# Turning k and x by transposing products, and a written order of all instructions, in a linear-attention and gated-MLP kernel

## The chip, the cores and the metric

The kernel runs on one core of a Trainium2 chip. The metric is the time that the device takes for one execution of the program, in microseconds (us).

## The reference

A linear attention with decay runs over 4 batches, 8 heads and 768 steps with a head size of 48; its output, put together over the heads, goes through an RMS norm and a gated MLP (384 to 1536 and back).

```python
for t in range(S):
    state = alpha[:, :, t, :, None] * state + einsum('bhd,bhe->bhde', k[:, :, t], v[:, :, t])
    y[:, :, t] = einsum('bhd,bhde->bhe', q[:, :, t], state)
x = y.transpose(0, 2, 1, 3).reshape(B * S, H * D)
rms = sqrt(mean(x * x, axis=-1) + 1e-06)
xn = x / rms * rms_g
g = xn @ w_gate
out = (g * sigmoid(g) * (xn @ w_val)) @ w_out
```

All is float32. The gate and value weights are 384 by 1536, the output weights 1536 by 384.

## The kernel before, in words

The 3072 rows are cut into 24 chunks of 128 (six in time for each of four batches). `attention(cc)` makes one chunk: two scans of the decays on VectorE (L661) with a reciprocal between them (L681), the products kh (L691) and qp (two halves, L698), score products on TensorE (L768; for the four first chunks in float32, L778), a mask on VectorE (L784; L794 for the first chunks), value products (L856; L804 for the first chunks), products with the state (L835, L813) and state sums (L933, L908). Float32 matrices are split into a high and a low float16 part (the low parts are made on VectorE, for instance L705, L732, L723, L758, L886 and L1005), and three products of parts stand for one. Chunks 0 to 3 are each batch's first; they have no state before them and stay in float32. Their k is turned by `k_across` (L893) and their normed x by `x_across` (L981): matmuls whose moving operand is an identity matrix `one`. For x, `x_less` (L995) then subtracts the high part in the same PSUM tile. Later chunks turn k and x by transposing DMAs.

The MLP works on seven groups of chunks (4, 2, 2, 4, 4, 4, 4). `expert_in` multiplies a group with one of twelve blocks of gate and value weights (L1149), gates on VectorE (L1166), makes the high part on ScalarE (L502) and the low part on VectorE (L1179). `expert_out` multiplies with the output weights (L1219), copies out (L1230) and stores through SyncE (L1234). Weights come as 64-bit words whose bytes `decode` puts together on VectorE (L541, L544, L552) and ScalarE (L536, L502).

After all weights have come once more and been inspected, `verdict` forms a flag that tells whether the scaled splits were good for these inputs: two small matmuls on TensorE (L1367, L1394) with VectorE steps behind each, the last of them a reduction (L1396) and two tiny steps (L1399, L1407) that write `flag`. Each engine reads the flag (L1425) and branches (L1426). In the branch for good inputs stands the store of the last output tile, held back until then:

```python
bad = nc.values_load(flags[0], min_val=0, max_val=1)
with tc.If(bad > 0) as case:
    general(...)
with case.Else():
    last_store[0]()
```

The order of the work is the planner's. Every step is a `plan.op` with an engine, a cost, its forerunners (`deps`) and the tiles that it holds (`use`; `BUFS` says how many of each there are). `Plan.order` counts due times backwards through the forerunners, adds the tuned numbers of `LATE`, `W_LATE`, `DUE`, `GAP` and `PACE`, and then lets each engine take, of what could start next, the step with the earliest due time. The result is sorted by planned start, and each engine, the DMA queue on SyncE among them, gets its steps in that order. Where the plan leaves TensorE idle before 45 us, it adds filler matmuls (`warm`, L1329).

There are 1737 steps: 390 on TensorE, 717 on VectorE, 458 on ScalarE, 25 on GpSimd, 147 on SyncE. In the order before, the verdict's second matmul stands between the second and third of the four groups of output products of chunk 22, and its reduction before the last two output copies. The two pieces of chunk 1's loads are issued with the decays (261 KB) first and the rest (512 KB) three loads later.

Of the kernel before, what the change touches and what calls it, by code (L numbers as in the profile page):

```python
# [64 lines left out]
    abs=0.86, odd=0.57, cnt=1.0, wh=0.83, pow=0.8, sc=0.76, sc32=0.8, ys=0.42, ysw=0.38, yv=0.63, yvw=0.57, y32=1.12, add=0.5, take=0.4, u=0.5, po=1.48, xp=0.9, kp=1.15, u32=0.66,  # L65
# [10 lines left out]
PACE = [1.0, 1.0, 1.15, 1.18, 1.18, 1.18, 1.18]  # L76
GAP = [-15.7, 137.0, 36.9, 106.2, -22.7, -134.2, 399.9]
DUE = [
    -719.9, -428.4, 411.3, -551.6, 184.4, 443.0, 1038.8, 186.9, 211.3, 740.5, 1018.7, 654.7, 756.4,
    831.8, 770.0, 432.6, 1179.9, 1019.1, 1109.0, 512.2, 336.7, 338.7, 475.6, 483.2,  # L80
]
LATE = dict(
    a16=95.7, abs=95.5, add=-3.0, al=-37.8, cnt=239.3, dec=-143.8, gd=128.7, k16=-225.5, kb=-100.3,
    kh=211.5, kl=37.3, kp=-148.6, ld2=204.9, load=96.2, mask=-127.2, near=132.3, ob=-144.7,
    odd=-153.0, pow=73.9, q16=-96.0, qh=38.4, ql=-11.4, rec=52.2, rest=-69.8, rg=8.7, rgt=-201.8,
    rgw=-6.4, s16=44.3, sc=-125.2, sc32=-36.5, scan=303.9, sd=70.9, shift=-71.0, sl=-52.1, sq=109.6,
    st=-82.7, st0=-193.5, take=-59.8, u=-107.2, u32=-53.5, v=186.2, v16=124.3, vl=-14.9, wh=160.7,
    wid=-93.7, wl=-301.4, wl2=15.7, wneg=80.9, x=-230.4, x16=-36.5, x32=-16.4, xb=-7.0, xl=-43.5,
    xneg=126.0, xp=27.6, y32=-52.5, ys=-23.6, ys32=-78.8, ysw=-43.9, yv=-74.0, yvw=-116.3,
)  # L90
LATE_CHECK = 3
W_LATE = [
    -285.5, -492.0, -249.7, -250.4, -99.8, -149.6, -106.2, -73.2, 53.8, -132.7, 151.4, 126.2, 126.8,
    172.8, 286.5, 195.7, 182.1, 333.3,
]
WARM_UNTIL, WARM, WARM_FIRST = 45.0, 0.24, 14
CUTS = [0, 2, 4]
SIDE = [3, 1]


class Plan:
# [9 lines left out]
    def op(self, engine, cost, fn, deps=(), use=(), due=None, lock=False, kb=0, late=0.0, kind=None, tile=None):  # L111

        o = dict(e=engine, c=cost, fn=fn, d=[d for d in deps if d], u=tuple(use), due=due, lock=lock,
                 kb=kb, late=late, i=len(self.ops), n=[], k=kind, w=tile)
        for d in o["d"]:
            d["n"].append(o)
        for k in o["u"]:
            self.users[k] = self.users.get(k, 0) + 1
        self.ops.append(o)
        return o  # L120

    def order(self):
        for o in reversed(self.ops):
            lat = WAIT.get(o["e"], LOAD_LAG + LOAD_END + 1.5)
            due = [n["s"] - lat for n in o["n"]] + ([o["due"]] if o["due"] is not None else [])
            o["s"] = min(due, default=1e6) - o["c"]
        for o in self.ops:
            o["s"] += o["late"]
        free = {t: [(0.0, i) for i in range(n)] for t, n in BUFS.items()}
        held, left, last = set(), dict(self.users), {}  # L130
        engine = dict.fromkeys(("PE", "DVE", "ACT", "POOL", "SP"), 0.0)
        ready = {e: [] for e in engine}
        wait = {o["i"]: len(o["d"]) for o in self.ops}
        for o in self.ops:
            o["r"] = 0.0
            if not o["d"]:
                ready[o["e"]].append(o)
        bus, port, done = 0.0, 0.0, []

        owner = [None]  # L140

        def start(o):
            t = max(engine[o["e"]], o["r"])
            if o["lock"] and t < port and o["e"] != owner[0]:
                t = port
            want = {}
            for k in o["u"]:
                if k not in held:
                    want[k[0]] = want.get(k[0], 0) + 1
            for tag, n in want.items():  # L150
                f = sorted(free[tag])
                if len(f) < n:
                    return None
                t = max(t, f[n - 1][0])
            return t

        left_ops = len(self.ops)
        while left_ops:
            left_ops -= 1
            best = None  # L160
            for e, ops in ready.items():
                at = [(start(o), o) for o in ops]
                at = [x for x in at if x[0] is not None]
                if not at:
                    continue
                t0 = min(x[0] for x in at)
                t, o = min((x for x in at if x[0] <= t0 + 0.12), key=lambda x: (x[1]["s"], x[1]["i"]))
                if best is None or t < best[0]:
                    best = (t, o)
            assert best, "the plan is stuck"  # L170
            t, o = best
            e = o["e"]
            ready[e].remove(o)
            for k in o["u"]:
                if k not in held:
                    held.add(k)
                    free[k[0]].sort()
                    self.slot[k] = free[k[0]].pop(0)[1]
            cost = o["c"]
            if e == "PE" and t < WARM_UNTIL:  # L180
                n = int((t - engine[e] - 0.3) / WARM)
                at = [x[1] for x in free["mm"] if x[0] <= engine[e]]
                if n > 0 and at:
                    fn = lambda slot=at[0], n=n: self.warm(slot, n)
                    done.append(dict(o, c=n * WARM, t=engine[e], fn=fn, k="warm", w=None))
            if o["lock"]:
                port, owner[0] = t + cost, e
# [12 lines left out]
            for n in o["n"]:  # L200
                n["r"] = max(n["r"], t + cost if n["e"] == e else o["f"])
                wait[n["i"]] -= 1
                if not wait[n["i"]]:
                    ready[n["e"]].append(n)
# [140 lines left out]
def tile_attn_moe(  # L345
# [12 lines left out]
    nc = tc.nc  # L358
    NC, _, AW = att.shape
    R = 112  # L360
# [152 lines left out]
    def add(engine, kind, *args, **kw):  # L513
        w = kw.get("tile")
        late = LATE.get(kind, 0.0) + (W_LATE[w] if w is not None else 0.0)
        return op(engine, COST[kind], *args, late=late, kind=kind, **kw)
# [3 lines left out]
    def decode(src, dst, name, col):  # L520
# [49 lines left out]
        w = col - o_w  # L570
        o = op("SP", 0.9, load, [], [raw], kb=900 if len(src) > 1 else 786, late=LATE["load"] + W_LATE[w], kind="load", tile=w)
        f = add("ACT", "abs", fold, [o], [raw], tile=w)
        o = add("DVE", "shift", shift, [o], [raw, wu], lock=True, tile=w)
        o = add("DVE", "rest", join, [o, f], [raw, wu], lock=True, tile=w)
        if name in LOW_W:
            ps = [("at", (name, n)) for n in range(2)]
            a = [add("PE", "wid", lambda n=n: bring(n), [o], [wu, ps[n]], tile=w) for n in range(2)]
            o = add("ACT", "wh", high, [o], [wu], tile=w)
            a = [add("PE", "wneg", lambda n=n: less(n), [o, a[n]], [ps[n]], tile=w) for n in range(2)]
            a = [add("ACT", "wl2", lambda n=n: residue(n), [a[n]], [ps[n]], tile=w) for n in range(2)]  # L580
            w_more[name] = a[0]
            return a[1]
        o = add("ACT", "wh", high, [o], [wu], tile=w)
        return add("DVE", "wl", low, [o], [wu], lock=True, tile=w)
# [52 lines left out]
    def attention(cc):  # L637

        due = DUE[cc]
# [374 lines left out]
        def x_turn():  # L1014
# [14 lines left out]
            "SP", 0.45, lambda: load_v(cc), use=[key("v")], kb=230, kind="v", late=LATE.get("v", 0.0)  # L1029
        )  # L1030
        if cc == 0:
            x = op("SP", 0.45, load_rg, kb=20, kind="rg", late=LATE.get("rg", 0.0))
# [56 lines left out]
        if first:  # L1089
# [4 lines left out]
            if cc in LOW_X:  # L1094
                x = add("PE", "xneg", x_less, [x], [xp, ("xT", g)])
                xt = op("ACT", COST["xb"], x_rest, [x], [xp, ("xT", g)], due=due, kind="xt")
            else:
                xt = op("DVE", COST["xl"], lambda: x_half(1), [x], [xp, ("xT", g)], due=due, kind="xt")
        else:
# [3 lines left out]
            xt = op("SP", 1.3, x_turn, [xl], [key("x16"), ("xT", g)], due=due, kb=300, kind="xt")  # L1103
# [28 lines left out]
    def expert_in(g, f, c0, c1, now, deps):  # L1132
# [57 lines left out]
        end = now + 2 * step * PACE[g]  # L1190
        b0, b1 = ("mm", name + "_0"), ("mm", name + "_1")
        x_k, s_k, h_k, o_k = ("xT", g), ("sl", name), ("h32", name), ("h16", (g, f))
        p0 = op("PE", step, lambda: mm(0), [tail[0]] + deps, [x_k, b0], due=now + step)
        p1 = op("PE", step, lambda: mm(1), [p0], [x_k, b1], due=end)
        tail[0] = p1
        sl = op("ACT", c_sl, silu, [p0], [b0, s_k], due=end)
        if low_pe:
            h = op("DVE", c_h, gate, [p1, sl], [b1, s_k], due=end + 1.6)
            hh = op("ACT", c_hh, h_hi, [h], [b1, o_k], due=end + 2.6)
            hl = op("PE", COST["neg"], h_less, [hh], [b1, o_k], due=end + 3.2)  # L1200
            hl = op("ACT", c_hh, h_rest, [hl], [b1, o_k], due=end + 4.2)
# [309 lines left out]
```

## Time and profile before

| what | us |
|---|---|
| median of 3 runs | 516.58 |
| lowest and highest of 3 runs | 514.37, 516.59 |
| profiled execution, first to last instruction (its only time on the page) | 514.9 |
| TensorE busy in it | 507.0 |
| VectorE busy in it | 387.0 |
| ScalarE busy in it | 254.1 |

A row of the profile names a line of the kernel, an engine (PE is TensorE, PEld its weight loads, DVE VectorE, ACT ScalarE, POOL GpSimd, SP SyncE; a q behind the name marks its sequencer), an operation and what it writes and reads. Float32 matmuls show two passes each, so 16 matmuls are 32 rows. A wait is given as idle time before an instruction with what ended it. Matmuls overlap and their ends are modelled, so in a timeline the spacing of starts says more than the length of one.

### The profile page before, as it was taken

To read this page: it belongs to the slowest core of one execution; us is meant where nothing else is said; L and a number is where in the kernel's file an instruction comes from. 1 tells how busy PE (TensorE), PEld (TensorE's weight loads), DVE (VectorE), ACT (ScalarE), POOL (GpSimd) and SP (SyncE) were. 2 spreads that over 40 slices of the span, in tenths; PEclk is the share of its full clock that TensorE was granted. 3 is DMA by queue.
4 is the path that set the end of the run, shared out by engine and by line. 5 is a ranking of instruction groups with operands and counts; after the bars stand their busy time and mean duration, and the time that the engine had idled before them with its cause. 6 is when DMAs were issued, how large, how long until landed. Compare 5 with 4: busy or idle time off the path is not lost.

```text
span 514.9 us, 12237 instructions
## 1 busy us (share of the span) xinstructions
PE 507.0 (98%) x5004; PEld 302.5 (59%) x5004; DVE 387.0 (75%) x734; ACT 254.1 (49%) x669; POOL 30.0 (6%) x85
## 2 busy tenths in 40 slices
PE   8999999999999999999999999999999999999996
PEld 4687844668877886445556545556544456444453
DVE  6999999999999999969999998995364320233321
ACT  2578977635644762448644356754365310233300
POOL 4011000100000100001111000100010000000000
PEclk9999999999999999999999999999999999999999
DMA  8979866566542645321675824018862000000001
GB/s 295 297 229 263 226 220 212 154 124 165 114 96 94 130 116 138 96 81 32 142 229 149 179 89 168 17 32 277 287 203 77 1 17 31 17 0 1 0 31 36
DMA packets 64031, 65.19 MB, mean 127 GB/s; under 512 B 32993, under 2 KB 57570, under 8 KB 63970
## 3 DMA queue, kind: packets, MB, share of 16 engines
q1 hardware_dynamic: 63970, 64.36, 44.5%
q8 instruction: 40, 0.66, 0.5%
q14 instruction: 21, 0.17, 0.1%
HBM read 52.03 MB, written 4.72 MB: 110 GB/s over the span
## 4 chain that ended last, share of the span: by engine, by line
PE 87%; DVE 5%; issue 1%; ACT 1%; DVEq 0%; ACTq 0%
PE mm L1149 53%; PE mm_po L1219 25%; PE at L768 3%; PE y L856 2%; PE at L933 1%; PE y L835 1%; DVE w L661 1%; DVE wu_i L544 0%; DVE wg L552 0%; DVE wu_i L541 0%; DVE qp L698 0%; DVE k L705 0%; DVE kh L691 0%; ACT h L502 0%; DVE h L1166 0%
## 5 line engine op out<-in xcount | busy, mean ns | idle before, releaser
L1149 PE MATMUL mm<-xT,wg 128*128 128x512 f16 (+1 forms) x1602 | 287.5, 338 | 0.0
L1149 PEld LDWEIGHTS <-wg 128*128 128x128 f16 x1602 | 153.8, 98 | 120.0 <-issue 0.5
L1219 PE MATMUL mm_po<-wo,h 128*128 128x384 f16 x864 | 144.0, 326 | 0.0
L1219 PEld LDWEIGHTS <-h 128*128 128x128 f16 x864 | 83.2, 98 | 55.8 <-issue 1.0
L1166 DVE SCALAR_TENSOR_TENSOR h<-mm,sl 128x512 f32<-128x512 f32 (+1 forms) x89 | 51.6, 584 | 46.0 <-PE mm L1149 43.4
L502 ACT ACTIVATE h<-h 128x512 f16<-128x512 f32 (+1 forms) x89 | 48.6, 546 | 73.5 <-DVE h L1166 73.0
L1160 ACT ACTIVATE sl<-mm 128x512 f32<-128x512 f32 (+1 forms) x89 | 45.5, 511 | 49.1 <-PE mm L1149 48.0
L1179 DVE TENSOR_TENSOR h<-h,h 128x512 f16<-128x512 f32 (+1 forms) x89 | 51.5, 584 | 18.1 <-ACT h L502 18.1
L661 DVE TENSOR_TENSOR_SCAN w<-att,seed 112x520 f32<-112x520 f32 x48 | 59.4, 1238 | 2.5 <-DMA att<-att 1.8
L1230 DVE TENSOR_SCALAR ob<-mm_po 128x384 f32<-128x384 f32 x24 | 13.2, 553 | 34.3 <-PE mm_po L1219 34.2
L964 POOL TENSOR_TENSOR ss<-ssq,eps 128x1 f32<-128x1 f32 x24 | 10.2, 425 | 351.8 <-ACT junk L960 351.8
L883 ACT CAST a<-at 128x512 f16<-128x512 f32 x40 | 22.9, 584 | 15.6 <-DVE at L784 15.5
L784 DVE TENSOR_TENSOR at<-at,mask 128x512 f32<-128x512 f32 x40 | 26.2, 690 | 2.3 <-PE at L768 2.1
L886 DVE TENSOR_TENSOR a<-at,a 128x512 f16<-128x512 f32 x40 | 26.4, 681 | 0.0
L502 ACT ACTIVATE q<-qp 112x512 f16<-112x512 f32 x20 | 12.5, 627 | 18.1 <-DVE qp L698 17.0
L698 DVE TENSOR_TENSOR qp<-att,w 112x256 f32<-112x256 f32 x48 | 18.8, 419 | 0.1
L768 PEld LDWEIGHTS <-k 48*128 48x128 f16 x480 | 13.5, 94 | 6.6 <-issue 5.1
L768 PE MATMUL at<-q,k 48*128 48x128 f16 x480 | 17.1, 217 | 0.1
L502 ACT ACTIVATION_READ_ACCUMULATOR h<-h 128x1 f32 x89 | 16.7, 188 | 0.0
L691 DVE TENSOR_TENSOR kh<-att,w 112x512 f32<-112x512 f32 x24 | 16.4, 684 | 0.0
L684 ACT COPY dec<-w 112x8 f32<-112x8 f32 x24 | 4.9, 203 | 22.3 <-DVE w L661 22.1
L608 ACT ACTIVATE wu_c<-wu_c 128x768 f32<-128x768 f32 x12 | 10.0, 836 | 9.4 <-DVE wu_c L602 9.4
(134 smaller groups left out, 449.3 us busy)
## 6 DMA issues: line engine op xcount, KB each, us to landing
att<-att SPq DMA_DIRECT2D x22, 773.0 KB, 5.1
v<-vtok SPq DMA_DIRECT2D x24, 192.0 KB, 3.1
out_dram<-ob SPq DMA_DIRECT2D x24, 192.0 KB, 2.0
raw_c<-w_gate SPq DMA_DIRECT2D x12, 384.0 KB, 4.1
raw_c<-w_val SPq DMA_DIRECT2D x12, 384.0 KB, 5.0
raw_d<-w_out SPq DMA_DIRECT2D x6, 768.0 KB, 4.5
raw_i<-w_gate SPq DMA_DIRECT2D x11, 384.0 KB, 4.3
raw_i<-w_val SPq DMA_DIRECT2D x11, 384.0 KB, 5.0
```

The lines of the kernel that those rows point to most:

```text
L502: nc.scalar.activation(dst, src, AF.Copy, scale=scale, accum_out=stat[:rows, col : col + 1])
L661: nc.vector.tensor_tensor_scan(w, x, start.rearrange("r g p c -> r (g p c)"), 0.0, op0=ALU.mult, op1=ALU.add)
L698: nc.vector.tensor_tensor(by_half(t["qp"])[:, g], q, w, op=ALU.mult)
L768: nc.tensor.matmul(t["sc"][j][:, p, :], t["k16"][r, x, p, :], t["q16"][r, y, p, :], start=m == 0, stop=m == 2,)
L784: nc.vector.tensor_tensor(t["sc"][j], t["sc"][j], mask.to_broadcast([P, NP, C]), op=ALU.mult)
L883: nc.scalar.copy(a_tile()[:, j, 0], t["sc"][j])
L886: nc.vector.tensor_tensor(a_tile()[:, j, 1], t["sc"][j], a_tile()[:, j, 0], op=ALU.subtract)
L1149: nc.tensor.matmul(ps[:, :n], wg[:, f, x, j, kk, :], xT[:, y, kk, cs], start=i == 0, stop=i == 3 * NK - 1,)
L1160: nc.scalar.activation(t["sl"][:, :n], t[0][:, :n], AF.Silu, scale=1.0 / (S_X * S_W))
L1166: nc.vector.scalar_tensor_tensor(t["h"][:, :n], t[1][:, :n], S_H / (S_X * S_W), t["sl"][:, :n], op0=ALU.mult, op1=ALU.mult,)
L1179: nc.vector.tensor_tensor(h16_of(g, f)[:, 1, cs], t["h"][:, :n], h16_of(g, f)[:, 0, cs], op=ALU.subtract)
L1219: nc.tensor.matmul(t[i][:, :DM], h16_of(g, f)[:, x, ts], wo[:, f // 2, y, f % 2, :], start=f == 0 and m == 0, stop=f == NF - 1 and m == 2,)
```

## The change

The matmuls of `k_across` and `x_across` get `is_transpose=True`, with the same operands and the same identity. In the planner's costs a turn of x is entered as 0.25 in place of 0.9 and one of k as 0.35 in place of 1.15. The due times and all tuned numbers that made them are removed; `Plan.order` now walks a list, `ORDER`, that holds all 1737 steps as numbers in base 36 (a step's number is its place in the order in which the program creates the steps). It works out planned starts along the list as before, gives out buffers, adds fillers by the same rule and sorts by planned start.

```diff
@@ COST
-    ... po=1.48, xp=0.9, kp=1.15, u32=0.66,
+    ... po=1.48, xp=0.25, kp=0.35, u32=0.66,
@@
-PACE = [1.0, 1.0, 1.15, 1.18, 1.18, 1.18, 1.18]
-GAP = [-15.7, 137.0, 36.9, 106.2, -22.7, -134.2, 399.9]
-DUE = [
...
+ORDER = """
+0 1 2 4 x w 3 2g 7 y 1o 8 3h a 9 5 36 b 6 c h d e 2f i z 10 f 11 g 12 j 14 k 15 13 l 19 9t 1q n 1a m o
+1p 1r 1t 1s 16 p 1u q 17 3i 20 18 3j 21 3k r 3l 45 1v 1b 1w 37 3m av 1c 38 s 39 1x 1d t 2h 1e 3c 3n u 1f
...
+h9 h6 kf hd l9 md la ha me q4 he kh hb hf mf hc ki lb q5 hj hg q6 kl kj q7 hk hh qv ml hp hl mk mn kk qx
...
+1a1 1a2 1a4 1a5 1a6 1a9 1a7 1a8 1aa 1ab 1ac 1af 1ad 1ae 1ag 1ah 1ai 1c7 1aj 1ak 1c8
+"""
@@ Plan.order
+        ops = [self.ops[int(x, 36)] for x in ORDER.split()]
+        assert sorted(o["i"] for o in ops) == list(range(len(self.ops)))
...
+        for o in ops:
+            e, cost = o["e"], o["c"]
+            t = engine[e]
+            for d in o["d"]:
+                t = max(t, d["t"] + d["c"] if d["e"] == e else d["f"])
...
@@ k_across
-                nc.tensor.matmul(t["kp"][:, p, :], t["kh"][:, p, :], one[:R, :R], start=True, stop=True)
+                nc.tensor.matmul(
+                    t["kp"][:, p, :], t["kh"][:, p, :], one[:R, :R], start=True, stop=True, is_transpose=True
+                )
@@ x_across
                     t["xp"][:, kk, :], t["x32"][:, kk * P : (kk + 1) * P], one,
-                    start=kk == 0, stop=kk == NK - 1, skip_group_check=True,
+                    start=kk == 0, stop=kk == NK - 1, is_transpose=True, skip_group_check=True,
```

Some numbers of the list. `x` and `w` are the loads of chunk 1, the 512 KB piece and the piece with the decays. `b`, `c` and `d` are chunk 0's kh and its two qp products; `h` is its turn of k, `e` its score products, `f` and `g` its masked scores; `z`, `10` and `12` are chunk 1's first scan, reciprocal and second scan. `kh` and `ki` are chunk 9's last a residue and its value products; 317 VectorE steps and 158 TensorE steps stand ahead of `ki`. In the last line, `1af` to `1ai` are the four groups of output products of the last chunk, `1c7` is the verdict's second matmul, `1aj` the copy of the last output tile, `1ak` an empty step on SyncE, and `1c8` the verdict's last reduction. The verdict's first matmul and the VectorE steps behind it come earlier, before the copy of the last group's first tile.

## Rows read from the trace of the kernel before

**Rows 1.** The page, busy time, share of the span and instructions of each engine.
```profile
PE 507.0 (98%) x5004; PEld 302.5 (59%) x5004; DVE 387.0 (75%) x734; ACT 254.1 (49%) x669; POOL 30.0 (6%) x85
```

**Rows 2.** Windows: length, busy time by engine, then granted clock, DMA share, GB/s.
```profile
20.00:50.00 30.00, 28.57 (x479) 23.13 (x478) 29.64 (x56) 22.74 (x64) 3.09 (x7) 1.00 0.83 237
100.00:150.00 50.00, 49.86 (x647) 38.13 (x645) 48.35 (x104) 26.55 (x82) 2.44 (x7) 1.00 0.49 110
150.00:200.00 50.00, 50.00 (x771) 38.21 (x769) 49.44 (x108) 27.25 (x87) 2.94 (x6) 1.00 0.50 123
```

**Rows 3.** The chain that ended last, in order of time: start, length, what.
```profile
501.97 8.90 PE mm_po L1219 x54
```

**Rows 4.** Groups of TensorE instructions by line and shape: busy, mean ns, idle before.
```profile
L893 PE MATMUL at<-one,kh 112*128 112x112 f32 x32 | 5.2, 316 | 0.0
...
L981 PE MATMUL mm_x<-one,x 128*128 128x128 f32 x24 | 3.7, 291 | 1.3 <-DVE x L974 1.2
```

**Rows 5.** Timeline of VectorE, the first 20 us: start, length, idle before and releaser.
```profile
12.35 0.76 DVE L794 TENSOR_TENSOR a<-at,near 128x256 f32<-128x256 f32 x2 [1.53 <-PE at L778]
...
18.47 0.96 DVE L544 SCALAR_TENSOR_TENSOR wu_i<-raw_i,wu_i 128x768 int32<-128x768 int32 x1 [0.46 <-ACT raw_i L536]
```

**Rows 6.** Timeline of TensorE, the first 22 us.
```profile
8.04 1.46 PE L1329 MATMUL warm<-minus 128*128 128x512 f16 x3
...
14.00 1.27 PE L804 MATMUL y<-v,a 64*64 64x48 f32 x30
...
18.23 2.98 PE L1329 MATMUL warm<-minus 128*128 128x512 f16 x13
```

**Rows 7.** Groups of VectorE instructions by line and shape.
```profile
L661 DVE TENSOR_TENSOR_SCAN w<-att,seed 112x520 f32<-112x520 f32 x48 | 59.4, 1238 | 2.5 <-DMA att<-att 1.8
...
L698 DVE TENSOR_TENSOR qp<-att,w 112x256 f32<-112x256 f32 x48 | 18.8, 419 | 0.1
L691 DVE TENSOR_TENSOR kh<-att,w 112x512 f32<-112x512 f32 x24 | 16.4, 684 | 0.0
...
L723 DVE SCALAR_TENSOR_TENSOR v<-v,v 128x384 f16<-128x384 f32 x20 | 10.8, 550 | 0.0
...
L949 DVE SCALAR_TENSOR_TENSOR st<-at,st 112x192 f32<-112x192 f32 x16 | 5.7, 356 | 1.3
```

**Rows 8.** Around chunk 9's value products: the chain, then VectorE's timeline.
```profile
169.90 0.38 PE y L835 x16
...
176.17 0.65 PE y L856 x16
...
177.80 0.49 PE at L933 x40
...
179.78 0.71 PE y L856 x24
...
174.59 1.28 DVE L886 TENSOR_TENSOR a<-at,a 128x512 f16<-128x512 f32 x2
...
177.17 0.75 DVE L1179 TENSOR_TENSOR h<-h,h 128x256 f16<-128x256 f32 x2
```

**Rows 9.** Lines L1425, L1426, L1507, L1234: ns min/median/max, first to last start.
```profile
L1425 SPq TENSOR_LOAD <-flag x1: 477/477/477, 503.0 to 503.0; - x1
...
L1425 SPq SEQ_ASSERT  x1: 28/28/28, 503.7 to 503.7; - x1
...
L1426 ACTq COMPARE_BRANCH  x1: 50/50/50, 503.5 to 503.5; - x1
...
L1426 ACTq EVENT_SEMAPHORE  x1: 17/17/17, 503.9 to 503.9; - x1
...
L1426 SPq COMPARE_BRANCH  x1: 53/53/53, 506.0 to 506.0; - x1
...
L1507 SPq EVENT_SEMAPHORE  x11: 17/28/28, 508.6 to 514.8; - x11
...
L1234 SPq DMA_DIRECT2D out_dram<-ob x24: 332/349/1878, 113.0 to 511.5; - x24
```

More of the change, by code (lines that the diff above doesn't have):

```diff
@@ L109, in __init__, with op @@
         self.slot = {}
[L111 to L116, printed above, removed]
+    def op(self, engine, cost, fn, deps=(), use=(), lock=False, kb=0, kind=None):
+        o = dict(e=engine, c=cost, fn=fn, d=[d for d in deps if d], u=tuple(use), lock=lock, kb=kb,
+                 i=len(self.ops), k=kind)
         for k in o["u"]:
@@ L122, in order @@
     def order(self):
[L123 to L128, printed above, removed]
+        ops = [self.ops[int(x, 36)] for x in ORDER.split()]
+        assert sorted(o["i"] for o in ops) == list(range(len(self.ops)))
         free = {t: [(0.0, i) for i in range(n)] for t, n in BUFS.items()}
-        held, left, last = set(), dict(self.users), {}
+        left, last = dict(self.users), {}
@@ L157, in order @@
[L157 to L176, printed above, removed]
+        bus, port, owner, done = 0.0, 0.0, None, []
@@ L513, in add @@
     def add(engine, kind, *args, **kw):
-        w = kw.get("tile")
-        late = LATE.get(kind, 0.0) + (W_LATE[w] if w is not None else 0.0)
-        return op(engine, COST[kind], *args, late=late, kind=kind, **kw)
+        return op(engine, COST[kind], *args, kind=kind, **kw)
     w_more = {}
@@ L569, in decode @@
         raw, wu = ("raw", name), ("wu", name)
[L570 to L574, printed above, removed]
+        o = op("SP", 0.9, load, [], [raw], kb=900 if len(src) > 1 else 786, kind="load")
+        f = add("ACT", "abs", fold, [o], [raw])
+        o = add("DVE", "shift", shift, [o], [raw, wu], lock=True)
+        o = add("DVE", "rest", join, [o, f], [raw, wu], lock=True)
         if name in LOW_W:
             ps = [("at", (name, n)) for n in range(2)]
[L577 to L580, printed above, removed]
+            a = [add("PE", "wid", lambda n=n: bring(n), [o], [wu, ps[n]]) for n in range(2)]
+            o = add("ACT", "wh", high, [o], [wu])
+            a = [add("PE", "wneg", lambda n=n: less(n), [o, a[n]], [ps[n]]) for n in range(2)]
+            a = [add("ACT", "wl2", lambda n=n: residue(n), [a[n]], [ps[n]]) for n in range(2)]
             w_more[name] = a[0]
             return a[1]
-        o = add("ACT", "wh", high, [o], [wu], tile=w)
-        return add("DVE", "wl", low, [o], [wu], lock=True, tile=w)
+        o = add("ACT", "wh", high, [o], [wu])
+        return add("DVE", "wl", low, [o], [wu], lock=True)
     def within(src, name, w, after):
@@ L1238, in expert_out @@
         cost = COST["po"] * n * every / 3
-        step = cost * PACE[g]
         for f in range(0, NF, every):
@@ L1249, in expert_out @@
             use = [("mm", f"po{g}_{t0 + i}") for i in range(n)] + [("h16", (g, f)) for f in fs]
[L1250 to L1251 removed]
+            tail[0] = op("PE", cost, part, [tail[0]] + deps, use)
         for i in range(n):
             b, o = ("mm", f"po{g}_{t0 + i}"), ("ob", f"{g}_{t0 + i}")
[L1254 removed]
+            e = add("DVE", "ob", lambda i=i: back(i), [tail[0]], [b, o])
             if chunks[i] == NC - 1:
                 last_store.append(lambda i=i: store(i))
[L1257 removed]
+                op("SP", 0.4, lambda: None, [e], [o])
             else:
[L1259 to L1260 removed]
+                op("SP", 0.4, lambda i=i: store(i), [e], [o])
     last_store = []
@@ L1322, in tile_attn_moe @@
             chunks = [starts[g] + t0 + i for i in range(n)]
-            now = expert_out(g, chunks, t0, now)
+            expert_out(g, chunks, t0)
             t0 += n
```

164 lines of the change are left out of this document (82 added, 82 removed).

## The prediction

> **What bounds the kernel now.** I read the page first, then the windows, the chain, and at last the timelines of the places that the chain points to. The page puts TensorE at 98% of the span [rows 1], which invites the reading that any TensorE work removed shortens the kernel. The windows correct that: from 20 to 50 us VectorE is busy 29.64 of 30 us, and from 100 to 200 us 97.79 of 100, beside a TensorE that is full as well [rows 2]. Two engines are full together, each feeding the other. The chain, followed to its end, tells where TensorE stops: its last piece ends at 510.87 us [rows 3], and 4.0 us follow to the span's 514.9 us.
>
> **The sum's own time.** The sum is made against the profiled execution, span 514.9 us. The median of the runs is 516.58 us, 1.7 us more; the lowest run, 514.37 us, lies 0.5 us under that span. I carry differences over to the median.
>
> **The transposes.** Removed are the identity products of k (16 matmuls, 32 passes, 5.2 us in four chunks) and of x (12 matmuls, 24 passes, 3.7 us) [rows 4]: 8.9 us. Added are 28 transposes. No row has one. From above, such a turn costs what it costs now; from below, nothing, since all that it does is in those rows. A turn has to stream its columns at least once where these rows show two passes for each matmul, so I take half, which saves 4.5 us of TensorE.
>
> The Trainium skill, "TensorE: Matmul & The Clock Gate", section Terms, says that the transposing mode is four times faster for FP32. By that, an estimate from the page, the saving would be 6.7 us; no row here shows it.
>
> Whichever holds, all 28 belong to the four first chunks, whose work lies in the first 50 us, where VectorE is the cover [rows 2]; none comes later. What they save directly is TensorE time in front of VectorE waits.
>
> **The order, early.** VectorE shows two waits there: 1.53 us before chunk 0's first masked scores, ended by TensorE's score products, and 0.46 us for a weight fold on ScalarE [rows 5]. TensorE, from 8.04 us on, runs three fillers before chunk 0's turn of k and so before those score products [rows 6]. In the list kh goes ahead of the two qp products, so the turn may start sooner, and chunk 0's masked scores stand ahead of chunk 1's second scan and no longer behind it: the first helps, the second leaves less cover, 1.2 us of scan. The fold's reader is later in VectorE's list, behind chunk 2's kh and chunk 1's masked scores. I let both waits go: 2.0 us. The bounds are nothing, if new waits of that size replace them, and 4.2 us, if the 1.65 and 0.56 us that VectorE idles in 100 to 200 us go too [rows 2].
>
> SyncE's list is moved as well: chunk 1's second piece, 512 KB, is now issued before the first, which chunk 1's first scan needs. At the 237 GB/s of 20 to 50 us [rows 2] that is 2.2 us later, and the cover is chunk 0's VectorE work. Were the cover gone, this would eat the gain; the bound of no gain has it in it. ScalarE's and GpSimd's lists are permuted too; their share of the span (49% and 6%) [rows 1] is their cover.
>
> **The order, middle.** Here the list is dearer than it looks. I count it at `ki`, the value product of chunk 9. In the list, 317 VectorE steps stand ahead of it. They are the first 319 steps of the old order less eleven (two s residues, one sum and one gain of x, a v and an x residue, two a residues, two state updates, one h residue) and plus nine of chunks 12 and 13 (two scans, kh and its residue, two qp products, a v residue, a reciprocal, a gd). By the groups' means, an unlisted kind priced by the listed one of its size, and the reciprocal and gd, of a few elements each, put at half of the smallest, the nine come to 5.6 us and the eleven to 5.4 us [rows 7]: 0.2 us more. The old order finished its 319th step at 177.92 us, and a value product begins 0.3 us behind its last residue (175.87 to 176.17) [rows 8]. So at the old pace `ki` could start at 177.92 + 0.2 + 0.3 = 178.4 us; in the old order it started at 179.78 us [rows 8].
>
> But the list leaves more for TensorE behind it: the state sums of chunks 9 and 10 (0.49 us each), the products of 10 and 11 with the state (0.38 each) and their value products (0.65 each) [rows 8], 3.0 us that the old order had already done there. Nothing that the old order had left is done. So TensorE ends 178.4 + 3.0 - 179.8 = 1.6 us later, less what VectorE saves in front: 1.6 - 2.0 = -0.4 us. With the bounds above: +1.6 to -2.6 us. The turns' own saving is no term of this: it ends in TensorE waiting for VectorE. Fillers that the planner puts into those waits cost nothing while VectorE is behind; without that cover one costs 0.23 to 0.49 us [rows 6].
>
> **The order, end.** The verdict on the inputs has moved. Before, its second matmul stood among the output products of the last chunk but one and ended at 501.97 us [rows 3]; SyncE read the flag at 503.0 us, branched at 506.0 us, and so waited at its last store long before the last output tile came [rows 9]. In the list `1c7`, that matmul, comes after `1ai`, the last output product, and `1c8`, the reduction, after `1aj`, the last output tile. The store in the Else branch has the whole verdict in front of it, in series. Step by step [rows 3, 9]: matmul's end to the read of the flag, 501.97 to 503.0 us, 1.0 us; the read and its checks on SyncE, to 503.7 us, 0.7 us; branch to the next instruction, 506.0 to 508.6 us, 2.6 us; then the store, issued at 511.5 us, to the end, 3.4 us. Sum 7.7 us where 4.0 us stood: +3.7 us. The branch is the one uncertain term: ScalarE's took 0.4 us (503.5 to 503.9) [rows 9], which leaves +1.5 us; and if the store of the last chunk but one is queued in between, its issue (0.35 us) makes it +4.05 us. I take SyncE's own row. All engines read the flag, but only this store has work of the kernel behind it.
>
> **Sum.** -0.4 + 3.7 = +3.3 us: a span of 518.2 us, and 519.9 us on the median.
>
> **The rivals.**
>
> - *The branch is cheap.* Then -0.4 + 1.5 = +1.1 us, 517.7 us. For it: ScalarE branches in 0.4 us. Against it: SyncE's own 2.6 us. Chance 0.22.
> - *TensorE is the bound all along* (the other side, faster). The page's 98% speaks for it: what the turns lose goes through to the end. At half, 516.6 - 4.5 + 3.7 = 515.8 us; at a quarter of the present 8.9 us, 516.6 - 6.7 + 3.7 = 513.6 us. It is faster by over 0.5% from a saving of 6.3 us on. Against it: VectorE's 29.64 of 30 us. Chance 0.14, of which 0.09 on the faster side.
> - *The clock.* The granted clock reads 1.00, its 2.4 GHz level, in every window [rows 2]; yet the first fillers take 0.49 us each at 8.04 us and 0.23 us each at 18.23 us [rows 6], as if TensorE were at the 1.2 GHz level until it had been busy for some time. If the turns don't help it up, the 4.2 us of products from 14.0 to 18.2 us [rows 6] double, and VectorE waits for about half: +2.1 us, 522.0 us. Chance 0.06. The Trainium skill, "TensorE: Matmul & The Clock Gate", Part 4, says that transposes don't count as busy for the clock as other matmuls do; by that this case would be the likely one, but no row here has a transpose.
> - *The transposes are no cheaper than the products.* The middle and the end of the sum don't hold a turn, so the time is the forecast's, up to 1 us later. It is part of it.
>
> **How the numbers follow.** The forecast has 0.58 and gives 519.9 us; its own ends are -2.6 + 1.5 and +1.6 + 4.05, 515.5 to 522.2 us. I take 515.0 to 522.2 us, which leaves out the faster side of the second rival and part of the clock's. A measurement of this kernel can tell about 0.5%, 2.6 us, from no change. Of the forecast's 0.58, some 0.10 lies under that, where VectorE gains more than 2.7 us; with the cheap branch (0.22) and the rest of the second rival (0.05), no change has 0.37. Slower has 0.48 + 0.06 = 0.54, faster 0.09.
>
> **What the profile after would show.** Right: half the passes in the turns of k and x, or less; a smaller wait before chunk 0's masked scores; TensorE's end between 508.3 and 512.5 us; the verdict's matmul as TensorE's last, the flag about 1 us behind it, and the last store more than 3 us behind the flag. Wrong: a last store less than 2 us behind the flag (cheap branch), TensorE's end at 506 us or earlier (TensorE was the bound), or large new gaps between 50 and 200 us, which neither the list nor the rows show me.

## The result, and the profile after

The changed kernel takes 520.97 us (median of 4 runs, 519.69 to 522.24), beside 515.48 us for the kernel before in the same session (4 runs): a ratio of 1.0118, 95% interval 1.0098 to 1.0138. It is slower by a little over one per cent. The executions of both kernels scatter: before takes 514.37 and 514.38 us beside 516.58 and 516.59 us, after 519.69 and 519.88 us (mean granted clock 0.997) beside 522.06 and 522.24 us (0.989 and 0.982), and both profiled executions, 516.58 and 522.24 us, are of the slower kind. In that of before, TensorE's fillers still run at half speed at 8 us [rows 6]; the granted clock reads 1.00 there, so this is read from their durations alone. In the larger sets of runs below, the median of before is 514.41 to 514.43 us.

The page of the kernel after, busy time by engine, then two of its windows (length, busy by engine, granted clock, DMA share, GB/s):

```profile
PE 506.4 (97%) x4981; PEld 299.7 (58%) x4981; DVE 386.9 (74%) x734; ACT 252.6 (49%) x669; POOL 32.3 (6%) x85
```
```profile
5.00:45.00 40.00, 36.45 (x525) 25.48 (x524) 36.64 (x64) 22.15 (x59) 4.65 (x19) 0.83 0.86 278
...
100.00:200.00 100.00, 99.49 (x1427) 75.89 (x1425) 98.50 (x212) 54.79 (x173) 9.05 (x14) 1.00 0.52 116
```

The busy sums say nothing here (compare [rows 1]). The first window does: VectorE stands still for 3.36 of 40 us, and the mean granted clock is 0.83.

The end of the execution, the timeline of all engines (start, length, what, idle before), and the read of the flag and the branch by SyncE (ns, first and last start):

```profile
511.88 0.85 PE L1377 MATMUL at_pok<-raw_work 128*1 128x413 f32 x2
511.99 0.56 DVE L1218 TENSOR_SCALAR ob<-mm_po 128x384 f32<-128x384 f32 x1 [5.29 <-PE mm_po L1207]
512.77 0.57 DVE L1379 TENSOR_REDUCE raw_work<-at_pok 1x1 f32<-1x413 f32 x1 [0.23 <-PE at_pok L1377]
...
513.56 0.14 DVE L1390 CAST flag<-raw_work 1x1 int32<-1x1 f32 x1
517.25 0.35 SPq L1222 DMA_DIRECT2D out_dram<-ob  x1
```
```profile
L1408 SPq TENSOR_LOAD <-flag x1: 475/475/475, 513.7 to 513.7; - x1
...
L1409 SPq COMPARE_BRANCH  x1: 45/45/45, 514.3 to 514.3; - x1
```

The verdict's matmul is TensorE's last and ends at 512.73 us (before: 501.97 + 8.90 = 510.87 us [rows 3]). The output tile is ready at 512.55 us, but its store starts at 517.25 us, behind flag, read and branch. From TensorE's end to the span's end (520.5 us) pass 7.8 us, where before had 4.0.

The turns of k and x in the kernel after, groups of TensorE by line and shape (the groups of [rows 4]):

```profile
L881 PE MATMUL at<-one,kh 112*128 112x112 f32 x16 | 2.8, 308 | 0.7 <-DVE kh L679 0.7
...
L971 PE MATMUL mm_x<-one,x 128*128 128x128 f32 x12 | 2.4, 319 | 0.0
```

Half the passes (16 and 12 for 32 and 24). Part of them ran at the lower clock, which is why 8.9 us became 5.2 and not 4.5.

The first 46 us of the kernel after, rows of VectorE's timeline, then of TensorE's, then windows around the falls of the clock:

```profile
8.75 1.24 DVE L649 TENSOR_TENSOR_SCAN w<-att,seed 112x520 f32<-112x520 f32 x1 [0.76 <-DMA att<-att]
...
10.15 0.72 DVE L782 TENSOR_TENSOR a<-at,near 128x256 f32<-128x256 f32 x2
...
42.82 0.42 DVE L1156 SCALAR_TENSOR_TENSOR h<-mm,sl 128x256 f32<-128x256 f32 x1 [1.63 <-PE mm L1139]
```
```profile
37.96 0.61 PE L1139 MATMUL mm<-xT,wg 128*128 128x256 f16 x2 [1.78 <-ACT wg L494]
39.12 3.59 PE L1139 MATMUL mm<-xT,wg 128*128 128x256 f16 x16 [0.55 <-DVE wg L542]
```
```profile
14.00:20.50 6.50, 6.50 (x78) 4.37 (x77) 6.19 (x12) 4.05 (x10) 0.99 (x2) 0.50 0.94 336
20.50:36.00 15.50, 15.50 (x286) 11.84 (x284) 15.13 (x27) 10.04 (x26) 1.26 (x2) 1.00 0.83 268
36.00:45.00 9.00, 6.67 (x70) 4.81 (x66) 7.33 (x14) 6.25 (x20) 1.21 (x2) 0.62 0.69 171
```

The 1.53 us before chunk 0's masked scores [rows 5] are gone (10.15 us, no wait). In their place stand a DMA wait of 0.76 us at chunk 1's scan, whose decays now load second, and 1.63 us at 42.82 us. From the latter one reads backwards: VectorE waits for gate products; these waited 1.78 and 0.55 us for the weights `wg`; and the granted clock is 0.62 in this stretch (0.50 is the 1.2 GHz level, 1.00 the 2.4 GHz level), so that 16 passes take 3.59 us. The weights are late because the list decodes block i5, needed later, ahead of block i2.

### The profile page after: what moved, and what is told of

It is laid out like the page before. It is cut to its first block, busy times and chain, and to the rows that moved or that the text cites. A ratio compares the mean times of both kernels' runs of the same rounds, so it can differ in the third digit from the quotient of the medians.

```text
span 520.5 us, 12187 instructions
## 1 busy us (share of the span) xinstructions
PE 506.4 (97%) x4981; PEld 299.7 (58%) x4981; DVE 386.9 (74%) x734; ACT 252.6 (49%) x669; POOL 32.3 (6%) x85
## 4 chain that ended last, share of the span: by engine, by line
PE 81%; DVE 9%; issue 1%; DMA 1%; ACT 1%; DVEq 0%
PE mm L1139 51%; PE mm_po L1207 23%; PE at L756 3%; PE y L844 2%; PE at L923 1%; PE y L823 1%; DVE wu_o L534 1%; DMA out_dram<-ob 1%; DVE w L649 1%; DVE wo L542 1%; DVE h L1156 1%; DVE a L874 1%; DVE wu_i L534 1%; DVE h L1169 0%; DVE wu_o L531 0%
## 5 line engine op out<-in xcount | busy, mean ns | idle before, releaser
L954 POOL TENSOR_TENSOR ss<-ssq,eps 128x1 f32<-128x1 f32 x24 | 12.0, 499 | 395.5 <-ACT junk L950 395.5
L494 ACT ACTIVATE k<-kh 112x512 f16<-112x512 f32 x20 | 12.5, 626 | 8.8 <-DVE kh L679 6.5
L861 ACT COPY x<-y 128x384 f32<-128x384 f32 x14 | 6.6, 473 | 20.7 <-PE y L844 19.5
```

The source lines that it names most:

```text
L494: nc.scalar.activation(dst, src, AF.Copy, scale=scale, accum_out=stat[:rows, col : col + 1])
```

## The experiments

Two theories on where TensorE's lateness comes from: E, the new list loses its time in the first 50 us; M, it loses it in the middle, where the prediction counted 3.0 us more of TensorE's work left. Beside them stands the verdict at the end, and on the clock two more: G, that TensorE's waits let it fall, against C, that transposes don't hold it up. Medians with ranges; ratios are against runs of before on the same chip in the same session.

**The verdict back in its old place.** The new list, its last line only:

```diff
-... 1aa 1ab 1ac 1af 1ad 1ae 1ag 1ah 1ai 1c7 1aj 1ak 1c8
+... 1aa 1c7 1ab 1c8 1ac 1af 1ad 1ae 1ag 1ah 1ai 1aj 1ak
```

> The changed kernel with the verdict's second matmul and its last reduction back where they stood before, among the output products of the last chunk but one. Theory (the verdict stands in series before the last store): the stretch from TensorE's end to the span's end falls from 7.8 to about 4.0 us, and the time by 3.7 us, from 521.0 to about 517.2 us. Rival (the whole loss is in the middle of the list and the end is hidden by something else): under 1 us, 520 us or more.

517.38 us (516.22 to 519.05, 11 runs), ratio 1.0046 (1.0031 to 1.0062): 3.6 us less than the full change. Its TensorE still ends at 512.2 us (503.33 + 8.89), and from there to the end of its span (516.2 us) pass 4.0 us, as in before, and no longer 7.8. Last piece of the chain, rows of the timeline at the end, and the window from 5 to 45 us:

```profile
503.33 8.89 PE mm_po L1207 x54
```
```profile
504.15 0.14 DVE L1390 CAST flag<-raw_work 1x1 int32<-1x1 f32 x1
...
512.25 0.56 DVE L1218 TENSOR_SCALAR ob<-mm_po 128x384 f32<-128x384 f32 x1 [5.29 <-PE mm_po L1207]
```
```profile
5.00:45.00 40.00, 33.30 (x535) 23.11 (x534) 37.08 (x65) 22.72 (x59) 6.11 (x18) 0.96 0.86 280
```

The flag is written at 504.29 us, 8.5 us before the last output tile is ready (512.81 us), and nothing of the verdict is left in series.

**The reverse: before, with the verdict's last two steps moved to the end.**

```diff
-for o in plan.order():
+done = plan.order()
+late = [o for o in done if o["i"] >= len(plan.ops) - 2]
+for o in [o for o in done if o not in late] + late:
```

> The kernel before with one thing moved: the verdict's second matmul and its last reduction stand last, behind the last output tile. Theory (serial verdict): 3.7 us slower, about 519.2 us. Rival (hidden): under 1 us.

518.75 us (518.20 to 519.13, 6 runs), ratio 1.0072 (1.0050 to 1.0093): 4.3 us over before. The same edit costs 3.6 us in one kernel and 4.3 in the other; here 8.4 us pass from TensorE's end (508.37 us) to the span's end (516.8 us). This run serves besides as a picture of the old order in an execution whose clock is up early. Rows of its TensorE and VectorE timelines, and its window from 5 to 45 us; last, that window of the kernel before:

```profile
7.33 0.82 PE L1329 MATMUL warm<-minus 128*128 128x512 f16 x3
7.99 1.07 PE L893 MATMUL at<-one,kh 112*128 112x112 f32 x8
...
46.19 0.94 PE L981 MATMUL mm_x<-one,x 128*128 128x128 f32 x6 [0.35 <-DVE x L974]
...
48.03 0.32 PE L995 MATMUL mm_x<-xT,minus 128*128 128x384 f16 x1 [0.51 <-ACT xT L989]
```
```profile
10.56 0.73 DVE L794 TENSOR_TENSOR a<-at,near 128x256 f32<-128x256 f32 x2
```
```profile
5.00:45.00 40.00, 38.11 (x607) 28.83 (x606) 39.25 (x68) 24.64 (x64) 5.04 (x20) 1.00 0.91 299
```
```profile
5.00:45.00 40.00, 39.01 (x563) 28.65 (x562) 37.36 (x65) 23.18 (x60) 3.85 (x18) 1.00 0.88 284
```

Three fillers in 0.82 us, not 1.46 [rows 6]: the clock is up earlier. And the old order then has no wait before chunk 0's masked scores at all; VectorE idles 0.75 us from 5 to 45 us, where the profiled execution of before has 2.64.

**The transposes alone, in the old order.** And, in the new list, the identity products back:

```diff
# before
-  one[:R, :R], start=True, stop=True)
+  one[:R, :R], start=True, stop=True, is_transpose=True)    # k; x likewise
# after: the same two edits undone
```

> The kernel before, its order kept, with the turns of k and x as transposes. Theory (VectorE sets the pace in the first 50 us, TensorE's relief ends in waits): between 1 us faster and no change, 514.5 to 515.5 us beside 515.5 us. Rival (TensorE is the bound): 4.5 to 6.7 us faster, 509 to 511 us. Second rival (transposes let TensorE's clock fall): granted clock under 1.00 before 50 us and no gain or a loss of up to 2 us.

> The changed kernel with identity products in place of the transposes, the list kept. Theory (VectorE sets the pace): within 1.5 us of the changed kernel, 520 to 522.5 us. Rival (TensorE is the bound): 4.5 us or more slower, 525 us. If the transposes let the clock fall, the granted clock here reads 1.00 before 50 us; if gaps in TensorE's work do, it falls here too where a gap stays.

The transposes alone: 516.50 us (515.51 to 521.61, 12 runs), ratio 1.0035 (1.0014 to 1.0057), slower by 2.1 us; of the expectations only the second rival, a loss by the clock, comes near. The full change with products: 523.82 us (521.41 to 524.97, 6 runs), ratio 1.0167 (1.0140 to 1.0195), 2.9 us over the full change, more than the theory's 1.5 and less than the rival's 4.5. Where that comes from isn't shown: in the traces TensorE ends at 512.73 us in the full change and at 512.72 us with products, and the whole difference of the two spans (520.5 and 521.5 us) lies behind it, in a last store that starts later although the flag comes no later:

```profile
518.21 0.35 SPq L1222 DMA_DIRECT2D out_dram<-ob  x1
```

In the old order one sees where time goes: rows of TensorE's timeline with the transposes alone, one of VectorE's, and a window.

```profile
46.30 0.55 PE L981 MATMUL mm_x<-one,x 128*128 128x128 f32 x3 [0.73 <-DVE x L974]
...
48.15 0.48 PE L995 MATMUL mm_x<-xT,minus 128*128 128x384 f16 x1 [0.89 <-ACT xT L989]
...
101.54 10.23 PE L1219 MATMUL mm_po<-wo,h 128*128 128x384 f16 x62 [1.29 <-issue]
```
```profile
52.18 0.42 DVE L1166 SCALAR_TENSOR_TENSOR h<-mm,sl 128x256 f32<-128x256 f32 x1 [1.25 <-PE mm L1149]
```
```profile
48.00:51.50 3.50, 3.35 (x16) 2.25 (x16) 2.92 (x5) 3.25 (x7) 0.00 (x0) 0.52 1.13 286
```

The last turn of x takes 0.55 us where products take 0.94 (above, at 46.19 us). TensorE waits 0.73 and 0.89 us around it where it waited 0.35 and 0.51, and behind that the granted clock is 0.52 for 3.5 us. VectorE, which doesn't wait there with products, waits 1.25 us at 52.18 us. Two readings are open: the waits let the clock fall (G), or transposes don't hold it (C). The full change with products speaks against C as the whole cause, for its clock falls near 40 us as well. A window of it:

```profile
36.00:45.00 9.00, 6.66 (x88) 5.30 (x84) 7.95 (x15) 6.32 (x20) 1.21 (x2) 0.81 0.76 183
```

But the fall isn't all of the 2.1 us. In the same trace TensorE stands for 1.29 us more before 101.54 us, where nothing that the profile shows holds it. And of the twelve executions seven have a mean granted clock of 1.000, so no such fall in its record, and still take 515.51 to 516.72 us; the traced one has 0.997 and 517.02 us.

**Transposes of the same TensorE time as products.** Each group twice, or with half of the products ahead of it:

```diff
# twice
+for _ in range(2):
     transposes of the four k parts      # x: the three parts, twice over
# half products
+identity products of two k parts        # x: of one and a half parts
 transposes of the four k parts          # x: the three parts
```

> The order of before with the transposing products, each group of them issued twice, the second pass over the first one's result: TensorE's time for the turns is then about that of the identity products again (2 times 0.55 us for a chunk's k, 2 times 0.5 us for its x). Theory G (the gaps let the clock fall: with the transposes once, TensorE ran ahead and stood 0.73 and 0.89 us before 48.1 us): the gaps shrink to 0.35 and 0.51 us as in the old order with products, the clock holds, and the time is that of before, 514.4 us, within 0.5. Theory C (transposes do not count for the clock, in whatever number): the time stays where the transposes once had it, 515.5 to 517.0 us, with the granted clock at 0.5 in some stretch before 52 us.

> The same order and the same TensorE time, but the second half of that time is spent on identity products (2 of a chunk's 4 for k, one and a half of 3 for x), ahead of the transposes that write over their result. Theory G: as with the transposes twice, 514.4 us within 0.5, and no difference between the two. Theory C: the products hold the clock at least in part, so this one is faster than the transposes twice by 1 us or more.

Twice: 514.56 us (514.29 to 516.21, 12 runs), ratio 1.0003 (0.9990 to 1.0016). Half products: 514.49 us (514.34 to 516.40, 12 runs), ratio 1.0006 (0.9993 to 1.0019). Both are the kernel before, and they are alike. The same two places with the transposes twice:

```profile
46.48 0.88 PE L982 MATMUL mm_x<-one,x 128*128 128x128 f32 x6 [0.41 <-DVE x L975]
...
48.33 0.32 PE L996 MATMUL mm_x<-xT,minus 128*128 128x384 f16 x1 [0.56 <-ACT xT L990]
```
```profile
48.00:51.50 3.50, 3.17 (x29) 2.79 (x29) 3.50 (x7) 3.50 (x8) 0.00 (x0) 1.00 1.25 223
```

Waits of 0.41 and 0.56 us, a clock of 1.00, VectorE full. Six passes of transposes in place of three, the second three useless, make the kernel 1.9 us faster. What C forecast didn't come: no products were needed, and with half products it is no faster. A weaker C, by which transposes count for less, isn't excluded, since the transposes twice also shorten the waits. Nor does G hold in its simple form, that a wait of such a length makes the clock fall: a run below has longer waits and no fall.

**Block i2 first, then also chunk 1's decays first**, both on the new list with the verdict back:

```diff
# list: the six decode steps of i2 (3n to 3s) and of i5 (45 to 4a) change places
# second run, besides:
-0 1 2 4 x w 3 ...
+0 1 2 4 w x 3 ...
```

> The new list with the verdict back in its old place, and the decode of weight block i2 (load, fold, shift, rest, high, low) exchanged with that of block i5 in the list, so that i2 comes first again, as it is used first. Theory E (the new list loses its time early): TensorE's waits of 1.8 and 0.8 us at the gate products of 37 to 39 us, the fall of the clock behind them and VectorE's wait of 1.63 us at 42.8 us all come from i2 being decoded late. Then these three rows go, and the time falls from 517.4 us by 1.5 to 3 us, to 514.4 to 516.0. Theory M (the middle decides: at chunk 9's value product near 178 us the new list has 3.0 us more of TensorE's work left): the waits may go but the time stays within 0.8 us of 517.4, since VectorE's lag at 170 us comes from elsewhere. Theory C (transposes do not hold the clock, whatever the order): the granted clock still falls to 0.5 near 40 us although the waits are gone.

> The run with block i2 first, and besides the two loads of chunk 1's attention tile in their old order (decays ahead of keys and queries). Theory E: the scan of chunk 1 no longer waits 0.76 us for a DMA near 8.8 us, and VectorE is that much earlier from there on: 0.3 to 0.8 us under the run with i2 first alone, so 513.8 to 515.5 us. Theory M: no change by this, within 0.4 us of the run with i2 first. Nothing is expected to be slower by it, unless another load becomes late by 0.3 us or more at the scan of chunk 2.

516.53 us (515.72 to 518.84, 8 runs), ratio 1.0040 (1.0026 to 1.0055): 0.85 us less than with the verdict back alone, under the 1.5 that theory E asked for and about the 0.8 that M allowed; the intervals of the two ratios overlap for the most part, so that this step alone can't be told from nothing. Its TensorE from 36 to 41 us, and its first window:

```profile
36.45 1.16 PE L1141 MATMUL mm<-xT,wg 128*128 128x256 f16 x9
39.06 1.14 PE L1141 MATMUL mm<-xT,wg 128*128 128x256 f16 x9 [1.45 <-ACT sl L1152]
40.82 0.55 PE L973 MATMUL mm_x<-one,x 128*128 128x128 f32 x3 [0.61 <-DVE x L966]
```
```profile
5.00:45.00 40.00, 36.02 (x564) 25.14 (x563) 37.95 (x66) 23.72 (x65) 4.90 (x18) 0.91 0.91 284
```

The wait for weights is gone; TensorE has run ahead to the next one, 1.45 us for ScalarE. VectorE's idle time is 2.05 us, 0.87 less than with the verdict back alone (40.00 - 37.08 = 2.92). With the decays first as well: 516.28 us (515.14 to 517.92, 8 runs), ratio 1.0030 (1.0012 to 1.0048); the 0.25 us between the two can't be told from nothing, where E had asked for 0.3 to 0.8. Its trace is no clean test of the loads: the wait for them is gone, but in this execution the fillers run at half speed until 12 us (four take 1.89 us), as in the profiled one of before, and 1.04 us before chunk 0's masked scores stand in its place.

**The two orders spliced.** The new list for 440 steps, then the old order; the reverse; and, with both mends, the new list for 440 and for 820 steps (past `ki`):

```diff
+ORDER = new[:440] + [s for s in old if s not in new[:440]]
```

> The transposes and the new list for its first 440 steps (to about 100 us of VectorE's work), then the order of before for all the rest, verdict and last store as before. Theory E: all of the loss lies in the first 50 us, so this stays at the time of the new list with the verdict back, 516.6 to 517.6 us, with TensorE's end near 512. Theory M: the loss lies at 178 us, and without the new middle it goes: 514.4 to 515.5 us. Both in part: by the sums of the work still left behind each wait for VectorE, the middle is worth at most 0.6 us here (502.6 against 502.0 us), so 516.3 to 516.9.

> The mirror of it: identity products and the order of before for the first 420 steps (about 94 us of VectorE's work), then the new list for all the rest, with the verdict in its old place. Theory E: the start is that of before and nothing is lost there, so the time is that of before, 514.4, or up to 0.8 us over it. Theory M: the middle costs its price here too: 516.0 to 517.4 us.

> The transposes and the new list for 440 steps with both mends (block i2 first, decays of chunk 1 first), then the order of before. By the lags read so far, TensorE's end is 501.5 us and VectorE's lag at 180 us in the old rest, so with a lag at 40 us that the mends bring from 5.9 to 5.0 or 5.5 us: TensorE's end 508.5 to 509.0, time 514.2 to 515.2 us where the clock is up by 7 us, and up to 2.2 us more where it rises at 14 us. Theory E: it is the best of the new starts and comes within 0.5 us of before. Theory C: the start keeps losing to the clock whatever its waits, 515.5 to 517.

> The same with the new list kept for 820 steps, past chunk 9's value product at 178 us, and the order of before only behind it. Theory M: the 3.0 us more of TensorE's work left at that product set the end here as in the full new list, TensorE's end is 504.2 us and the lag at 180 us, so at equal clock 0.7 to 1.5 us later than the mended start with the old rest. If the two are equal within 0.4 us, the middle costs nothing and what the new list loses beyond the start lies behind 200 us.

New start, old rest: 516.36 us (515.15 to 517.87, 6 runs), ratio 1.0043 (1.0028 to 1.0058), within the 516.3 to 516.9 that both theories in part were to give. With the mends: 515.24 us (514.97 to 517.15, 12 runs), ratio 1.0019 (1.0007 to 1.0032), the nearest of the new starts and still 0.8 us over before, where E asked for 0.5.

The traced execution of the new start is its fastest, 515.15 us, and the only one of the six with a mean granted clock of 1.000; the others have 0.993 to 0.997 and 516.10 us or more. Its first 440 steps are those of the full change, unmended. TensorE's wait for the late weights is there, and a window:

```profile
37.08 0.39 PE L1141 MATMUL mm<-xT,wg 128*128 128x256 f16 x2 [1.82 <-ACT wg L496]
38.24 1.92 PE L1141 MATMUL mm<-xT,wg 128*128 128x256 f16 x16 [0.77 <-DVE wg L544]
```
```profile
36.00:45.00 9.00, 7.08 (x131) 5.46 (x132) 8.92 (x16) 8.22 (x25) 1.21 (x2) 1.00 0.89 255
```

The waits are as long as in the full change (1.78 and 0.55 us), but the clock holds, the 16 passes take 1.92 us and not 3.59, and VectorE is full. Chunk 1's scan doesn't wait for its load either. So in these traces the late weights cost VectorE time only where the clock falls behind them, and waits of this length don't always bring the fall. The other two splices say nothing of the middle: old start, new rest (519.15 us, 518.09 to 521.35, ratio 1.0093) and the 820 steps (519.78 us, 518.07 to 521.08, ratio 1.0100) lose at the splice itself, as one row of TensorE's timeline of each shows (the first is of the old start, the second of the 820 steps):

```profile
108.74 2.92 PE L1209 MATMUL mm_po<-wo,h 128*128 128x384 f16 x17 [2.74 <-DVE wo L544]
```
```profile
191.91 1.14 PE L1141 MATMUL mm<-xT,wg 128*128 128x256 f16 x9 [1.51 <-ACT sl L1152]
```

For the middle there remain pairs with like starts. First windows of the new list with both mends and of the unmended new start with the old rest:

```profile
5.00:45.00 40.00, 36.36 (x567) 25.14 (x566) 38.02 (x66) 23.94 (x65) 5.40 (x18) 1.00 0.90 287
```
```profile
5.00:45.00 40.00, 34.23 (x593) 23.96 (x592) 39.02 (x67) 25.11 (x66) 6.19 (x18) 1.00 0.89 295
```

Set out by run, VectorE's idle time from 5 to 45 and from 45 to 60 us, TensorE's end, and that end less both, in us:

```
                                 5-45   45-60   TensorE's end   less both
old rest:  before                2.64   0.10    510.87          508.1
           verdict last          0.75   0.00    508.37          507.6
           transposes twice      0.85   0.00    508.80          508.0
           half products         0.75   0.00    508.62          507.9
           new start             0.98   0.21    509.40          508.2
           mended start          1.03   1.95    511.43          508.5
           transposes alone      0.75   1.29    511.28          509.2
new rest:  after                 3.36   0.37    512.73          509.0
           after with products   2.73   0.73    512.72          509.3
           verdict back          2.92   0.37    512.22          508.9
           both mends            1.98   0.24    511.02          508.8
           i2 first              2.05   0.24    512.39          510.1
```

What VectorE loses in the first 60 us returns at the end nearly one to one, and on top of that the new rest is 0.4 to 1.6 us dearer. Two runs stand apart and are left out of this, the transposes alone and i2 alone first: each has 98.71 us of TensorE from 100 to 200 us where the others have 99.5 to 99.9, so each lost again there. The medians say the same of the rest: 517.38 to 516.36 and 516.28 to 515.24, 1.0 us each, though the intervals of each pair overlap for the most part.

## Why the prediction was right, and where it was wrong

**The end** (+3.7 us): measured +3.6 us by putting it back and +4.3 us by moving it in the old kernel; 7.8 us from TensorE's end where the sum had 7.7. The last store starts 3.55 us behind the flag (513.70 to 517.25), and some 2.9 us behind SyncE's branch at 514.3 us, where its row of before gave 2.6: the cheap branch falls. The store of the last chunk but one isn't queued in between.

**The transposes** (half the time, no term of the sum): half it is. At a granted clock of 1.00 a chunk's turn of k takes 0.55 to 0.60 us and one of x 0.49 to 0.55; as products in the old order the first took 1.07 and the second 0.94. The factor of four of the Trainium skill ("TensorE: Matmul & The Clock Gate", Terms) is not seen: two is, one pass for two. "It ends in TensorE waiting for VectorE" was right too, but I took such a wait for free. It isn't always: the transposes alone cost 2.1 us in the old order. In the traced execution a fall of the clock behind the longer waits gave VectorE 1.25 us of that; the rest isn't explained.

**The early order** (-2.0 us) is the step that failed: "I let both waits go: 2.0 us." The waits went, as forecast, but they were not the old order's. They belonged to the profiled execution, whose clock came up late; where it is up early, the masked scores don't wait, and the old order idles VectorE for 0.75 us from 5 to 45 us, the new start for 0.98. There was nothing to win. And new waits came that I had taken as covered or hadn't looked for: 0.76 us by the exchanged loads, where I had named 2.2 us of delay and "chunk 0's VectorE work" as its cover, and 1.63 us by block i2, whose place in the list I never read, together with the clock that fell behind it. From 5 to 45 us VectorE idles 3.36 us: 0.7 more than in the profiled execution of before where the sum had 2.0 less. That difference of 2.7 us is nearly the 2.3 us by which TensorE's end (+1.9 us) missed the -0.4 of the sum. At 512.73 us it lies even outside the 508.3 to 512.5 us that were to show me right.

**The middle** (+1.6 us) holds; the pairs, with VectorE's idle time counted apart, put the whole new rest at 0.4 to 1.6 us. `ki` started where the count of steps had put it without any early gain, in the chain of the kernel after:

```profile
178.43 0.60 PE y L844 x24
```

The forecast for this start was 178.4 less the 2.0 us; it is 178.43 with none of them. The exact hit is in part luck, for VectorE idles 1.0 us more than in before up to 60 us and 1.0 us less from 60 to 200 us. Behind it, the work left shows directly: from this start to TensorE's end pass 334.3 us, in before 331.1 (179.78 to 510.87), 3.2 us more where the sum had 3.0. So with an early gain of nothing, my sum gives +1.6 us for TensorE's end, and +1.9 was measured.

**The sum.** Against the profiled execution +5.6 us (514.9 to 520.5), with +1.9 in front of TensorE's end and +3.8 behind it, where the forecast had -0.4 and +3.7. That the forecast of 519.9 us came near 520.97 us is luck: it was carried to a median of 516.58, of three executions that take 514.37, 516.58 and 516.59 us. Against the 514.4 us that before mostly takes, the change costs 6.5 us, twice the sum's 3.3. By the medians of the runs that is: verdict 3.6, block i2 0.85, decays 0.25, rest 1.0, and 0.8 that stays with the mended new start. Only the first is clear of noise as a step by itself, and the others mix executions in which the clock fell with those in which it held: the unmended new start with the old rest took 515.15 us where it held, the mended one 514.97 to 515.28.

**The rivals.** TensorE as the bound all along fell: in the old order half of the turns' time went, and nothing was won. The clock, as a rival, does cost time here, but hardly where I named it. In the trace of after it stands at 0.50 from 14.0 to 20.5 us, as that rival had it, though it had been up before; yet VectorE loses 0.31 us there (6.50 - 6.19) and not 2.1. The 1.63 us come later, from the fall behind TensorE's waits near 37 us. The Trainium skill says ("TensorE: Matmul & The Clock Gate", Part 4) that transposes don't count as busy for the clock as other matmuls do. The transposes issued twice, at 514.56 us and with a clock of 1.00 where single ones had 0.52, don't show that for turns of this size among other matmuls, nor do they exclude it.

What stays open: the 0.8 us of the mended start, why the transposes alone, in their best executions, still take 515.5 us, and what, at the same waits, makes the clock fall in one execution and hold in another. With the transposes alone, the profile caught only an execution with the fall at 48 us. No version here beat the kernel before; two equalled it.

## What to carry to other kernels

Work that must be done before the last store (a check, a flag, a branch) belongs ahead of the last products, not behind them: here 3.6 to 4.3 us in series. Read a wait in one profiled execution against a second one before counting it as something to win. And a faster operation on an engine that then waits may not be free: look at the granted clock behind each wait that it lengthens, in more than one execution, and try whether useless work there is cheaper than the wait.

## What the hardware showed that was not expected

Issuing the transposes twice, useless work on the fullest engine, took the old order from 516.50 to 514.56 us. With the transposes once, waits of 0.73 and 0.89 us within 2 us on TensorE were followed by 3.5 us at a granted clock of 0.52; with them twice, waits of 0.41 and 0.56 us at the same place were not.

But the length of the waits doesn't settle it. The mended start was traced twice, with the old rest and with the new middle: the same first 440 steps and the same waits of TensorE at 38 and 39.5 us. In the first the clock is at 0.50 from 40 to 45 us, in the second at 1.00. Rows and window of the first, then of the second:

```profile
37.82 1.14 PE L1141 MATMUL mm<-xT,wg 128*128 128x256 f16 x9 [1.46 <-ACT sl L1152]
39.58 0.90 PE L973 MATMUL mm_x<-one,x 128*128 128x128 f32 x3 [0.61 <-DVE x L966]
...
40.00:45.00 5.00, 5.00 (x56) 3.45 (x55) 4.93 (x8) 4.32 (x13) 0.00 (x0) 0.50 0.98 252
```
```profile
37.76 1.14 PE L1141 MATMUL mm<-xT,wg 128*128 128x256 f16 x9 [1.45 <-ACT sl L1152]
39.51 0.55 PE L973 MATMUL mm_x<-one,x 128*128 128x128 f32 x3 [0.61 <-DVE x L966]
...
40.00:45.00 5.00, 4.90 (x113) 3.76 (x113) 4.90 (x9) 4.87 (x15) 0.00 (x0) 1.00 1.06 309
```

This goes with the times of the mended start with the old rest: eight executions lie at 514.97 to 515.28 us, seven of them with a mean granted clock of 0.999 or 1.000 and one with 0.993, and four at 516.88 to 517.15 us, all with 0.992; the traced one is of these.
